# Another order of units in a fused attention, MoE and FFN kernel, with both opening AV products of a head pair at its first AV unit

## The chip, the cores and the metric

The kernel runs on one core of a Trainium2 chip. The metric is the device time of one execution in microseconds: the median of three executions of the kernel before is 460.26 us (459.25, 460.26 and 460.54). The profile is of one further execution.

The engines are TensorE (PE; its weight loads are listed apart as PEld), VectorE (DVE), ScalarE (ACT), GpSimd (POOL) and SyncE (SP), which here only issues DMA transfers. Each works through its own list of instructions in order; between lists, semaphores order the work. A DMA that SP issues has the engine name SPq in the trace, one that ScalarE issues ACTq.

## The reference

Three layers follow each other. Attention: 2 batches of 8 heads, 768 tokens of 64 dimensions; a key takes part in a query's softmax only where both have the same six-bit hash, and the bits are signs of projections.

```
q_bits = (einsum('bhsd,dk->bhsk', q, proj) > 0);  k_bits likewise
mask   = q_bucket[:, :, :, None] == k_bucket[:, :, None, :]
scores = where(mask, scale * q @ k.T, -1e9)
attn   = exp(scores - max) / (sum + 1e-09);   out = attn @ v
```

Then a soft mixture of experts on the 1536 x 512 result (8 experts with 4 slots each, `w1` 512 x 1024 and `w2` 1024 x 512 per expert, softmax of `x @ phi` over the tokens and over the slots), and a feed-forward layer `h = x @ w_in; g = h - tanh(h); g @ w_out` with 2048 hidden columns.

## The kernel before

Attention goes over the heads in eight pairs, `i` = 0 to 7. Each pair is cut into small units of work, and each unit is one Python function that issues its instructions on all the engines it needs. What is written first is first on every engine: the program's order is five lists of unit names. START runs once ahead of the pair loop, FIRST in the pass of pair 0, STEP in passes 1 to 5, STEP2 in pass 6, LAST in pass 7; the lists MOE, RUN and LOOP that follow are not touched. A pass of the loop finishes one pair and begins the next two, by a fixed offset for each unit name.

The units that matter here, with their lines:

- `const.0` (L169) loads the table `ct`, which also holds the identity matrix; `const.1` (L172) loads `proj` on ScalarE's DMA queue and two small things; `h0` to `h3` (L381) copy the queries and keys of a pair, where `xq` and `xk` have been loaded, into QA and KA.
- `b0` computes the hash bits of a pair: TensorE products L355, VectorE L361. `wk..` and `wq..` put them into QA and KA (ScalarE L369, VectorE L371). `l0` to `l3` make the low parts KB and QB (for pairs behind the first on VectorE, L419).
- `m` is one chunk of the pass that finds each query's largest masked score: TensorE `pm` (L447), then a VectorE maximum (L449). There are 18 per pair. `fa`, `fb` (or `f2` for both at once) close it: VectorE L454, a TensorE transpose `pc` (L457), VectorE L460 and L461, and a DMA that puts the row into QA. The scores of the pair need that row.
- `s0` and `s1` are chunks of scores for one head of the pair: TensorE `pst` (L508, two matmuls per block, QA with KA and QB with KB), ScalarE's exponential `e` (L511), and on GpSimd (for one head of the last pair VectorE) the running sum `es` (L521, L523).
- `a` is one AV unit: products of `e` and the values (L538) into the two tiles `pav`, of 512 and of 256 columns. Nine units belong to a pair. The first product into a tile is a constant product of `zrw` and `vzw` that sets the whole tile (L532); the tile of 512 columns gets it in the first unit, the one of 256 columns in the third.
- `xr`, `x2` and `x3` (L552, L574, L603) bring the result of a pair into its place; `lg` makes the MoE's logits of a pair (TensorE L617, VectorE L620, GpSimd L626 and L627).
- `wl` loads a piece of `w_in`, `wc` converts one: ScalarE L184, and VectorE L188, L197, L202. `lp` loads one piece of the MoE's weights (L249, `w` in the trace) into a ring of slots; slots are added as the tiles of attention are given back. The loop opens the last of them when all scores have been issued, the logits of pair 6 have been made, and pair 7's AV has begun.
- `keep.n` issues n small TensorE products (L720, `warm`) that nobody reads; each shows as two records.

All tiles in PSUM for scores, maxima and small products come from one pool of six buffers.

Of the kernel before, what the change touches and what calls it, by code (L numbers as in the profile page):

```python
# [10 lines left out]
F32 = mybir.dt.float32  # L11
# [8 lines left out]
B, H, S, D = 2, 8, 768, 64  # L20
# [4 lines left out]
P = 128  # L25
# [34 lines left out]
PARTS = ((0, 512), (512, S))  # L60
# [5 lines left out]

START = ("oi.0 qk.0 h1.0 const.1 const.0 warm.4 const.2 keep.1 hp3.0 keep.3 h0.0 wl.0 b0.0 wk0a.0 hp2.0 kc.0 wq0v.0 wl.0 "
        "m.0 keep.1 m.0 m.0 qk.1 l1.0 m.0 wk1a.0 m.0 m.0 m.0 m.0 keep.1 m.0 v.0 wq1a.0 m.0 keep.3 m.0 m.0 keep.3 m.0 "  # L70
        "v1.0 d.0 h2.1 h3.1 l0.0 m.0 fa.0 m.0 m.0 m.0 h1.1 v.1 oi.1 keep.1 b0.1 m.0 l3.0 fb.0 h0.1 wc.0 wq0a.1 wl.0 "
        "kc.1 s0.0 keep.1 l2.0 oi.2 wl.0 qk.2 fz.0 wk1a.1 s0.0 wk0v.1 s0.0 wc.0 a.0 wq1a.1 s0.0 v2.0 wc.0 s0.0 s0.0").split()
FIRST = ("wc wc lp lp a a a a a a a g0 g1 h1 fy wl m vy g2 l0 a a l1 l2 s0 h0 s0 s1 m m s1 s1 v m wl m h3 qk m m d m m "
        "xe s1 h2 b m m s0 m e wl lg m s1 m s1 m s0 lp e s0 wl xr v1 lp m x3 x2 m s1 s0 s1 e m s1 lp lp s0 s0 f2 s0 s0 "
        "wc s1 e").split()
STEP = ("a a a a a a a a wc a d g0 l0 fy h1 g1 wc l1 g2 h0 h3 lp l2 vy m m wl s0 m lp s0 s1 v xe m m qk m s0 m e xr b m "
        "h2 x2 m m v1 wl s0 lp m s1 lp s0 m m lg x3 s1 m m s1 m s0 m wc e s0 s0 s1 s1 s1 m wl s0 s1 s0 lp lp e s1 f2 e "
        "s1 wl").split()
STEP2 = ("m m a a a a a a vy s0 a a a a fy g1 l1 m s0 s0 m a m s1 h1 m s0 s1 m m m s1 g0 wl m xe d l0 xr m m v s0 v1 a a "
        "e s1 g2 m l2 a a m lp m e e lp lp s0 wl s1 wl lp b x2 qk wc s1 m m s0 v2 e lp m s1 wc h2 a a a f2 wc h3 lp h0 "  # L80
        "fz lp s0 wl s0 s1 x3 s1 lg lp").split()
LAST = ("a a s0 a lp xe a a a s0 lp lp a a lp s0 s0 lp s0 s1 s1 s0 s1 xr s0 s1 s1 lp s1 s1 lp a a lp a s0 x2 s1 s0 lg "
        "x3 s1 a").split()


MOE = ("k.1 k.1 k.1 F.0 F.1 R.1 T.0 R.0 W.0 F.2 X.0 W.1 T.2 k.1 T.1 k.1 wm.2 R.2 H.0 F.3 wm.3 X.1 k.1 T.3 W.2 H.1 X.2 "
# [55 lines left out]
def body(ctx: ExitStack, tc: tile.TileContext, q, k, v, proj, phi, w1, w2, w_in, w_out, cst, out, dbg=None):  # L142
    nc = tc.nc
    const = ctx.enter_context(tc.tile_pool(name="const", bufs=1))
# [6 lines left out]
    lg = const.tile([P, B * KT, NS], F32, name="lg")  # L151
# [101 lines left out]
    def attention():  # L253
# [23 lines left out]
        pav_p = actx.enter_context(tc.tile_pool(name="pav_p", bufs=1, space=PSUM, reuse_waits="tile"))  # L277
# [34 lines left out]
        mx, zr, vz, es, pav, xtu, rsT, rinv, uses = {}, {}, {}, {}, {}, {}, {}, {}, {}  # L312
# [213 lines left out]
        def av_unit(i, n, e2):  # L526
            cs = SEQ[n]
            k, (c0, c1) = len(cs) - 1, PARTS[len(cs) - 1]
            if cs[0] == 0:
                if k == 0:  # L530
                    pav[i] = [pav_p.tile([P, w], F32, tag=f"pav{w}", name="pav") for w in (512, S - 512)]
                nc.tensor.matmul(pav[i][k], vz[i], zr[i].rearrange("r c j -> r (c j)")[:, c0:c1], start=True, stop=False,  # L532
                                 skip_group_check=True)
                if k == 1:
                    del zr[i], vz[i]
            for j, c in enumerate(cs):
                for h in ((k + j) % 2, (k + j + 1) % 2):
                    nc.tensor.matmul(pav[i][k][64 * h:64 * h + 64, :], tv[i][:, h, c, :], e2[h][:, j * 256:j * 256 + c1 - c0],  # L538
                                     start=False, stop=c == KT - 1, tile_position=(0, 64 * h), skip_group_check=True)
# [160 lines left out]
        def unit(w, i):  # L700
# [15 lines left out]
            elif w in ("warm", "keep"):  # L716

                w_ = 256 if w == "warm" else P
                for _ in range(i):
                    nc.tensor.matmul(wt[0][:32, :w_], wz[:, :32] if w == "warm" else ident[:, :32], wz if w == "warm" else ident, start=True, stop=True)  # L720
            elif w == "b0":
                bits0(i)
            elif w[:2] in ("wq", "wk"):
                rows0(i, "qk".index(w[1]), int(w[2]), w[3:])
            elif w == "lp":
                if i > 4:
                    load_pieces(1)
            elif w == "const":
                (lambda: consts(projb), lambda: consts2(phiB, projb, blk), lambda: consts3(phiB))[i]()
            elif w in ("s0", "s1"):  # L730
                s_next(i, int(w[1]))
            elif w == "a":
                if queue and queue[0][2][1] is not None:
                    av_unit(*queue.popleft())
            elif w == "ap":
                while queue and queue[0][0] < i:
                    av_unit(*queue.popleft())
            elif w == "e":
                if len(d0.get("n", ())) < 4 and {("x3", 3), ("lg", 3)} <= done:
                    d0.setdefault("n", []).append(i)  # L740
                    disp0(len(d0["n"]) - 1)
            else:
                units[w](i)
# [3 lines left out]
        nc.vector.memset(wz, 0.0)  # L747
        for w in START:
            u, n = w.split(".")
            unit(u, int(n))  # L750
        del wt[:]
        for i in range(NPR):
            for u in FIRST if i == 0 else STEP if i <= WIDE else STEP2 if i < last else LAST:
                n = i + role.get(u, role.get(u[0], 0))
# [30 lines left out]
        while queue:  # L785
            av_unit(*queue.popleft())
# [547 lines left out]
    with tc.manual_schedule():  # L1334
# [20 lines left out]
        r = nc.values_load(flag, min_val=0, max_val=1)  # L1355
# [58 lines left out]
```

## Time and profile before

| | |
|---|---|
| median of 3 executions | 460.26 us |
| profiled execution: device time, span | 460.77 us, 459.0 us |
| TensorE busy | 437.5 us, 95% of the span |
| VectorE, ScalarE, GpSimd busy | 325.5, 272.9, 286.5 us |
| mean granted TensorE clock | 0.976 |

The span is what the trace covers; 1.77 us of the device time lie outside it. The program's stretches are: up to 10.6 us loads and the hash bits of pair 0; to 28.3 us its maxima; to 53.2 us its scores along with the maxima of pair 1; to 244.8 us the rest of the pair loop; then the MoE to some 306 us, while its weights stream in; then the feed-forward layer to the end. A window row gives, for a stretch, the busy time of each engine with its number of instructions, the granted TensorE clock as a share of full speed, the share of the DMA engines' time and the GB/s moved.

### The profile page before, as it was taken

How to read it: one execution, taken by the hardware profiler on the slowest of the kernel's cores; microseconds unless marked ns; L12 is line 12 of the kernel's file. 1: busy time of each engine (PE TensorE's matmuls, PEld its weight loads, DVE VectorE, ACT ScalarE, POOL GpSimd, SP SyncE). 2: the span in 40 equal slices, each digit the busy share in tenths (PEclk: the TensorE clock that was granted, in tenths of full speed). 3: DMA queues.
4: the chain of work that ended last, by engine and by line, in shares of the span. 5: the costliest groups of instructions: out<-in, count | busy, mean ns of one | idle time of the engine just before them, and what ended most of it. 6: DMA issues, size and time to landing. Idle time of an engine off the chain costs nothing. (4 is left out here: it accounts for less than half of the span.)

```text
span 459.0 us, 7553 instructions
## 1 busy us (share of the span) xinstructions
PE 437.5 (95%) x2621; PEld 300.1 (65%) x2621; DVE 325.5 (71%) x585; ACT 272.9 (59%) x525; POOL 286.5 (62%) x287
## 2 busy tenths in 40 slices
PE   6877999999999999999999999999999999999994
PEld 2544568575866768466766444657777778888883
DVE  3789999999999888276354358489998976444541
ACT  4568747667695756355631111288988878665751
POOL 5399849889797968949870100046878774535350
PEclk9678999999999999999999999999999999999999
DMA  6736372636455270846649999990000003000004
GB/s 180 189 116 199 84 211 88 180 95 158 143 145 174 59 196 21 311 156 272 231 191 423 416 421 420 417 413 17 2 0 3 0 0 139 0 2 0 1 2 144
DMA packets 18166, 71.33 MB, mean 155 GB/s; under 512 B 3492, under 2 KB 4616, under 8 KB 13000
## 3 DMA queue, kind: packets, MB, share of 16 engines
q1 hardware_dynamic: 17976, 70.75, 44.3%
q8 instruction: 23, 0.38, 0.4%
q14 instruction: 23, 0.19, 0.1%
q10 hardware_dynamic: 144, 0.02, 0.0%
HBM read 60.09 MB, written 3.15 MB: 138 GB/s over the span
## 5 line engine op out<-in xcount | busy, mean ns | idle before, releaser
L511 ACT ACTIVATE e<-pst 128x512 f32<-128x512 f32 x144 | 78.5, 604 | 39.0 <-PE pst L508 36.1
L521 POOL TENSOR_TENSOR es<-es,e 128x512 f32<-128x512 f32 x73 | 93.6, 1293 | 3.3 <-ACT e L511 2.5
L449 DVE TENSOR_REDUCE mx<-pm 128x1 f32<-128x512 f32 x144 | 89.7, 679 | 7.0 <-PE pm L447 6.8
L508 PE MATMUL pst<-QA,KA 128*128 128x256 f32 (+1 forms) x192 | 66.3, 359 | 3.9 <-ACT QA L369 1.3
L538 PE MATMUL pav<-e,tv 128*64 128x512 f32 (+1 forms) x384 | 66.6, 491 | 0.0
L508 PE MATMUL pst<-QB,KB 128*128 128x256 f32 (+1 forms) x192 | 63.1, 343 | 0.0
L447 PE MATMUL pm<-KA,QA 96*128 96x512 f32 x192 | 55.2, 381 | 3.8 <-DVE QA L371 3.0
L1229 DVE SCALAR_TENSOR_TENSOR ph<-win,ph 128x512 f32<-128x512 f32 (+1 forms) x64 | 35.7, 558 | 32.3 <-ACT win L1224 30.9
L1260 POOL TENSOR_TENSOR split<-win,split 128x512 fp32r<-128x512 f32 x31 | 44.6, 1439 | 14.5 <-ACT split L1255 14.5
L521 POOL TENSOR_TENSOR es<-e 128x512 f32<-128x512 f32 x30 | 39.4, 1313 | 19.6 <-PE pr L552 19.5
L1281 PE MATMUL po<-w,split 128*128 128x512 f32 x128 | 51.0, 398 | 0.0
L1279 PE MATMUL po<-w,split 128*128 128x512 f32 x128 | 50.6, 396 | 0.0
L1280 PE MATMUL po<-w,split 128*128 128x512 f32 x128 | 50.4, 394 | 0.0
L1260 POOL TENSOR_TENSOR ghl<-win,ghl 128x256 fp32r<-128x256 f32 x32 | 24.3, 758 | 37.0 <-ACT ghl L1255 37.0
L447 PEld LDWEIGHTS pm<-KA,QA 96*128 96x128 f32 x192 | 35.2, 207 | 18.5 <-issue 9.3
L538 PEld LDWEIGHTS pav<-e,tv 128*64 128x64 f32 x384 | 25.7, 136 | 31.4 <-issue 24.8
L508 PEld LDWEIGHTS pst<-QA,KA 128*128 128x128 f32 x192 | 36.9, 192 | 13.5 <-ACT e L511 5.0
L1224 ACT ACTIVATE win<-ph 128x512 f32<-128x512 f32 (+1 forms) x64 | 30.8, 481 | 22.7 <-PE ph L1217 22.1
L1230 DVE SCALAR_TENSOR_TENSOR win<-win,ph 128x512 f32<-128x512 f32 (+1 forms) x64 | 35.5, 555 | 9.1 <-ACT win L184 0.5
L1225 ACT ACTIVATE win<-win,ct 128x512 f32<-128x512 f32 (+1 forms) x64 | 39.6, 619 | 2.1
L508 PEld LDWEIGHTS pst<-QB,KB 128*128 128x128 f32 x192 | 37.1, 193 | 3.1
L1281 PEld LDWEIGHTS po<-w,split 128*128 128x128 f32 x128 | 24.0, 188 | 7.8 <-POOL split L1260 2.8
(230 smaller groups left out, 814.0 us busy)
## 6 DMA issues: line engine op xcount, KB each, us to landing
w<-in_moe_w_dram SPq DMA_DIRECT2D x32, 1024.0 KB
raw<-in_moe_w_in_dram SPq DMA_DIRECT2D x16, 512.0 KB
w<-in_moe_w_out_dram SPq DMA_DIRECT2D x8, 1024.0 KB
xq<-in_q_dram SPq DMA_DIRECT2D x8, 384.0 KB
xk<-in_k_dram SPq DMA_DIRECT2D x8, 384.0 KB
tv<-in_v_dram SPq DMA_DIRECT2D x8, 384.0 KB
out_dram<-win SPq DMA_DIRECT2D x12, 256.0 KB
QB<-QA SPq DMA_DIRECT2D x10, 192.0 KB
```

The lines of the kernel that those rows point to most:

```text
L447: nc.tensor.matmul(pm[:, j * 256:j * 256 + c1 - c0], QA[s][h][:96, c * P:(c + 1) * P], KA[s][h][:96, c0:c1], start=True, stop=True)
L449: nc.vector.reduce_max(m, pm.rearrange("p (c k) -> p c k", c=len(cs)), axis=AX.X)
L508: nc.tensor.matmul(pst[:, j * 256:j * 256 + c1 - c0], K[h][:, c * P:(c + 1) * P], Q[h][:, c0:c1], start=x == 0, stop=x == 1)
L511: nc.scalar.activation(e, pst, AF.Exp, scale=0.125)
L521: eng.tensor_tensor(q[0], y, e, ALU.add)
L538: nc.tensor.matmul(pav[i][k][64 * h:64 * h + 64, :], tv[i][:, h, c, :], e2[h][:, j * 256:j * 256 + c1 - c0], start=False, stop=c == KT - 1 ...
L1225: nc.scalar.activation(w, z, AF.Square, bias=ct[:, C_QA:C_QA + 1])
L1229: nc.vector.scalar_tensor_tensor(self.ph[p], z, Q_C, self.ph[p], ALU.mult, ALU.mult)
L1260: (eng or nc.gpsimd).tensor_tensor(gl[p], g, gh[p].bitcast(F32), ALU.subtract)
L1279: nc.tensor.matmul(po, gh[p][:, us], wo.half(f, 0), start=f == 0, stop=False)
L1280: nc.tensor.matmul(po, gh[p][:, us], wo.half(f, 1), start=False, stop=False)
L1281: nc.tensor.matmul(po, gl[p][:, us], wo.half(f, 0), start=False, stop=f == NF - 1)
```

## The change

All five lists are written in another order. Each holds the same units as before. In the AV unit, both constant products now stand in the first unit of a pair, one behind the other, instead of in the first and the third. Lines behind L530 move up by two (the AV products are L536, the logits L615, `keep` L718). Two lines of a list show the kind of edit; the other lists change alike.

```diff
-START = ("oi.0 qk.0 h1.0 const.1 const.0 warm.4 const.2 keep.1 hp3.0 keep.3 h0.0 wl.0 b0.0 wk0a.0 hp2.0 kc.0 wq0v.0 wl.0 "
...
+START = ("const.0 oi.0 qk.0 hp3.0 warm.4 const.1 const.2 b0.0 wl.0 h1.0 h0.0 hp2.0 wk0a.0 wq0v.0 keep.1 wl.0 m.0 wk1a.0 "
...
-LAST = ("a a s0 a lp xe a a a s0 lp lp a a lp s0 s0 lp s0 s1 s1 s0 s1 xr s0 s1 s1 lp s1 s1 lp a a lp a s0 x2 s1 s0 lg "
-        "x3 s1 a").split()
+LAST = ("a a a a lp xe a s0 s0 lp a a a s0 lp s0 s1 s1 s1 s0 lp xr s0 a a lp x2 x3 s1 s1 lp s1 s0 s0 s0 lp s1 s1 s1 lg "
+        "lp a a").split()
...
-            if cs[0] == 0:
-                if k == 0:
-                    pav[i] = [pav_p.tile([P, w], F32, tag=f"pav{w}", name="pav") for w in (512, S - 512)]
-                nc.tensor.matmul(pav[i][k], vz[i], zr[i].rearrange("r c j -> r (c j)")[:, c0:c1], start=True, stop=False,
-                                 skip_group_check=True)
-                if k == 1:
-                    del zr[i], vz[i]
+            if n == 0:
+                pav[i] = [pav_p.tile([P, w], F32, tag=f"pav{w}", name="pav") for w in (512, S - 512)]
+                for p, (r0, r1) in zip(pav[i], PARTS):
+                    nc.tensor.matmul(p, vz[i], zr[i].rearrange("r c j -> r (c j)")[:, r0:r1], start=True, stop=False, skip_group_check=True)
+                del zr[i], vz[i]
```

The lists of instructions that come of it differ on every engine. TensorE, the maxima of pair 0: the products of the hash bits (`pb`), the maxima (`pm`), the products that nobody reads (`warm`) and the first transpose (`pc`), before:

```order
L355 MATMUL pb<-xk,projb 32x384 x2
L447 MATMUL pm<-KA_135,QA_131 128x512
L720 MATMUL warm<-ct 32x128
L447 MATMUL pm<-KA_135,QA_131 128x512
L447 MATMUL pm<-KA_135,QA_131 128x256 x2
L447 MATMUL pm<-KA_135,QA_131 128x512 x2
L447 MATMUL pm<-KA_135,QA_131 128x256 x2
L447 MATMUL pm<-KA_135,QA_131 128x512 x2
L720 MATMUL warm<-ct 32x128
L447 MATMUL pm<-KA_135,QA_131 128x256 x2
L447 MATMUL pm<-KA_135,QA_131 128x512
L720 MATMUL warm<-ct 32x128 x3
```

And now, the same stretch:

```order
L355 MATMUL pb<-xk,projb 32x384 x2
L718 MATMUL warm<-ct 32x128
L447 MATMUL pm<-KA_135,QA_131 128x512 x2
L447 MATMUL pm<-KA_135,QA_131 128x256 x2
L447 MATMUL pm<-KA_135,QA_131 128x512 x2
L718 MATMUL warm<-ct 32x128 x6
L447 MATMUL pm<-KA_135,QA_131 128x256 x2
L718 MATMUL warm<-ct 32x128
L447 MATMUL pm<-KA_135,QA_131 128x512 x2
L718 MATMUL warm<-ct 32x128
L447 MATMUL pm<-KA_135,QA_131 128x256 x2
L718 MATMUL warm<-ct 32x128 x3
```

Up to the close of pair 0's maxima, nine of these small products stood behind `pb` before, and 13 do now, six of them in one row.

VectorE, the stretch behind the close of pair 0's maxima, as a difference; `cl` and `win` are a conversion of `w_in`, KA_136 the bit rows of pair 1:

```order
 L197 SCALAR_TENSOR_TENSOR cl<-cg,cl 128x512
 L202 SCALAR_TENSOR_TENSOR win<-raw,cl 128x512
+L493 TENSOR_TENSOR vt<-pv,blk 4x128
 L371 TENSOR_SCALAR KA_136<-pb,ct 24x384 x2
-L188 TENSOR_SCALAR cl<-raw 128x512
-L197 SCALAR_TENSOR_TENSOR cl<-cg,cl 128x512
-L202 SCALAR_TENSOR_TENSOR win<-raw,cl 128x512
-L493 TENSOR_TENSOR vt<-pv,blk 4x128
 L188 TENSOR_SCALAR cl<-raw 128x512
 L197 SCALAR_TENSOR_TENSOR cl<-cg,cl 128x512
```

Three conversions stood ahead of the close of pair 1's maxima, two stand there now; the third is made with the rest of them in pass 5.

TensorE where a pair's AV begins (here pair 0), before:

```order
L457 MATMUL pc_602<-ct_61,mh_600 12x128
L532 MATMUL pav_616<-zrw_129,vzw_130 128x512
L538 MATMUL pav_616<-e_328,tv_228 64x512
L538 MATMUL pav_616<-e_443,tv_228 64x512
L538 MATMUL pav_616<-e_348,tv_228 64x512
L538 MATMUL pav_616<-e_455,tv_228 64x512
L532 MATMUL pav_617<-zrw_129,vzw_130 128x256
L538 MATMUL pav_617<-e_464,tv_228 64x256
```

And now:

```order
L457 MATMUL pc_594<-ct_61,mh_592 12x128
L532 MATMUL pav_610<-zrw_129,vzw_130 128x512
L532 MATMUL pav_611<-zrw_129,vzw_130 128x256
L536 MATMUL pav_610<-e_328,tv_198 64x512
L536 MATMUL pav_610<-e_437,tv_198 64x512
L536 MATMUL pav_610<-e_340,tv_198 64x512
L536 MATMUL pav_610<-e_452,tv_198 64x512
L536 MATMUL pav_611<-e_490,tv_198 64x256
```

The constant product of 256 columns has moved from between two AV units to behind the other constant product. In passes further on, where scores and AV units alternate, the lists also gather AV units into longer rows.

## Rows read from the trace of the kernel before

**Rows 1.** Stretches, core 0; engine busy us (instructions), granted clock, DMA share, GB/s.

```profile
28.30:53.20 24.90, 19.91 (x84) 13.05 (x83) 23.56 (x41) 19.65 (x35) 22.93 (x19) 0.88 0.56 163
53.20:244.80 191.60, 190.83 (x1251) 126.51 (x1251) 148.53 (x272) 115.90 (x220) 155.19 (x157) 1.00 0.52 167
79.43:105.56 26.13, 26.13 (x168) 17.86 (x167) 24.46 (x45) 18.26 (x35) 22.84 (x24) 1.00 0.51 144
239.50:306.00 66.50, 63.98 (x607) 34.22 (x602) 36.53 (x68) 15.27 (x35) 7.02 (x18) 1.00 1.01 417
```

**Rows 2.** VectorE's groups, 28.3 to 53.2 us; count, busy us, mean ns, idle before.

```profile
L197 DVE SCALAR_TENSOR_TENSOR cl<-cg,cl 128x512 uint32<-128x512 uint32 x3 | 2.1, 696 | 0.5 <-ACT cg L184 0.3
L202 DVE SCALAR_TENSOR_TENSOR win<-raw,cl 128x512 uint32<-128x512 uint32 x3 | 2.1, 686 | 0.1
L188 DVE TENSOR_SCALAR cl<-raw 128x512 uint32<-128x512 uint32 x3 | 2.0, 681 | 0.0
```

**Rows 3.** One stretch of pass 5, columns as in the first group.

```profile
180.00:186.00 6.00, 6.00 (x37) 5.20 (x36) 3.60 (x8) 5.39 (x11) 5.56 (x6) 1.00 0.49 173
```

**Rows 4.** ScalarE's timeline, start: start us, duration us, instruction, idle before.

```profile
3.72 0.84 ACT L381 ACTIVATE QA<-xq 64x768 fp32r<-64x768 f32 x1 [1.71 <-DMA xq<-in_q_dram]
3.72 0.37 ACTq L172 DMA_DIRECT2D projb<-in_proj_dram  x1
4.70 0.85 ACT L381 ACTIVATE KA<-xk 64x768 fp32r<-64x768 f32 x1
```

**Rows 5.** TensorE's timeline, start of the program.

```profile
6.39 0.71 PE L355 MATMUL pb<-xq,projb 128*32 128x384 f32 x1
```

**Rows 6.** TensorE's timeline and one stretch, in the maxima of pair 0.

```profile
19.43 1.34 PE L720 MATMUL warm<-ct 128*32 128x128 f32 x6
10.24:20.48 10.24, 9.89 (x31) 6.33 (x32) 8.33 (x14) 6.36 (x9) 1.56 (x3) 0.50 0.91 241
```

**Rows 7.** TensorE's timeline, pair 1 ahead of and in its first AV units.

```profile
100.19 0.41 PE L447 MATMUL pm<-KA,QA 96*128 96x512 f32 x1
100.44 0.29 PE L508 MATMUL pst<-QA,KA 128*128 128x256 f32 x1
100.57 0.28 PE L508 MATMUL pst<-QB,KB 128*128 128x256 f32 x1
...
105.56 0.47 PE L532 MATMUL pav<-zrw,vzw 128*128 128x512 f32 x1
105.96 1.94 PE L538 MATMUL pav<-e,tv 128*64 128x512 f32 x8
107.83 0.39 PE L532 MATMUL pav<-zrw,vzw 128*128 128x256 f32 x1
108.15 1.08 PE L538 MATMUL pav<-e,tv 128*64 128x256 f32 x8
```

**Rows 8.** TensorE's weight loads in the same AV units.

```profile
106.45 0.14 PEld L538 LDWEIGHTS pav<-e,tv 128*64 128x64 f32 x2 [0.29 <-issue]
106.88 0.14 PEld L538 LDWEIGHTS pav<-e,tv 128*64 128x64 f32 x2 [0.29 <-issue]
```

**Rows 9.** TensorE's timeline, a maximum ahead of the small products of `x2`.

```profile
119.69 0.50 PE L447 MATMUL pm<-KA,QA 96*128 96x512 f32 x1
120.03 0.49 PE L574 MATMUL prt<-ct,rsT 128*128 128x128 f32 x3
```

**Rows 10.** GpSimd, SP's queue and TensorE around the weight stream's restart and end.

```profile
233.83 1.72 POOL L521 TENSOR_TENSOR es<-es,e 128x512 f32<-128x512 f32 x1
236.73 0.60 POOL L626 TENSOR_TENSOR lgt<-lgt 128x192 f32<-128x192 f32 x1 [1.18 <-DVE lgt L620]
...
238.03 2.48 SPq L249 DMA_DIRECT2D w<-in_moe_w_dram  x5
...
294.72 1.07 PE L1000 MATMUL po<-w,hold 128*32 128x256 f32 x16 [0.36 <-DMA w<-in_moe_w_dram]
```

**Rows 11.** TensorE's longest wait, 53.2 to 244.8 us: releaser, us, times, longest.

```profile
PE pc L457 <- DVE mh L454: 0.9, 1, 0.9
```

More of the change, by code (lines that the diff above doesn't have):

```diff
@@ L65 @@
 RING, HOLD = (4, 1, 3, 4, 3, 2, 3, 1), 4
-START = ("oi.0 qk.0 h1.0 const.1 const.0 warm.4 const.2 keep.1 hp3.0 keep.3 h0.0 wl.0 b0.0 wk0a.0 hp2.0 kc.0 wq0v.0 wl.0 "
-        "m.0 keep.1 m.0 m.0 qk.1 l1.0 m.0 wk1a.0 m.0 m.0 m.0 m.0 keep.1 m.0 v.0 wq1a.0 m.0 keep.3 m.0 m.0 keep.3 m.0 "
-        "v1.0 d.0 h2.1 h3.1 l0.0 m.0 fa.0 m.0 m.0 m.0 h1.1 v.1 oi.1 keep.1 b0.1 m.0 l3.0 fb.0 h0.1 wc.0 wq0a.1 wl.0 "
-        "kc.1 s0.0 keep.1 l2.0 oi.2 wl.0 qk.2 fz.0 wk1a.1 s0.0 wk0v.1 s0.0 wc.0 a.0 wq1a.1 s0.0 v2.0 wc.0 s0.0 s0.0").split()
@@ L73 @@
[L73 to L78, printed above, removed]
@@ L79 @@
-STEP2 = ("m m a a a a a a vy s0 a a a a fy g1 l1 m s0 s0 m a m s1 h1 m s0 s1 m m m s1 g0 wl m xe d l0 xr m m v s0 v1 a a "
-        "e s1 g2 m l2 a a m lp m e e lp lp s0 wl s1 wl lp b x2 qk wc s1 m m s0 v2 e lp m s1 wc h2 a a a f2 wc h3 lp h0 "
-        "fz lp s0 wl s0 s1 x3 s1 lg lp").split()
-LAST = ("a a s0 a lp xe a a a s0 lp lp a a lp s0 s0 lp s0 s1 s1 s0 s1 xr s0 s1 s1 lp s1 s1 lp a a lp a s0 x2 s1 s0 lg "
-        "x3 s1 a").split()
+START = ("const.0 oi.0 qk.0 hp3.0 warm.4 const.1 const.2 b0.0 wl.0 h1.0 h0.0 hp2.0 wk0a.0 wq0v.0 keep.1 wl.0 m.0 wk1a.0 "
+        "kc.0 m.0 m.0 v.0 m.0 m.0 keep.3 l0.0 keep.3 m.0 keep.1 m.0 wq1a.0 m.0 qk.1 keep.1 h2.1 oi.1 h3.1 m.0 keep.3 "
+        "m.0 wl.0 l1.0 m.0 d.0 m.0 v1.0 keep.1 fa.0 m.0 m.0 m.0 v.1 b0.1 l3.0 m.0 m.0 h0.1 m.0 fb.0 h1.1 wl.0 wc.0 "
+        "wk1a.1 wq1a.1 s0.0 l2.0 fz.0 wq0a.1 s0.0 v2.0 kc.1 qk.2 s0.0 wk0v.1 keep.1 oi.2 wc.0 s0.0 a.0 wc.0 s0.0 s0.0").split()
@@ new lines @@
+FIRST = ("a a a a a a a wc lp fy g0 g1 m l0 l1 wc lp a wl m a vy g2 s0 h1 l2 h3 h0 v qk s1 s0 m s1 m xe d h2 m s0 m m e "
+        "wl s1 m xr wl v1 m s1 m m s0 b lg m s0 m s1 s1 m m s0 e s0 s0 m s1 x2 e m e wl lp s1 lp m s1 x3 f2 lp s0 lp wc "
+        "s1 s0").split()
+STEP = ("d a wc g0 a l0 g1 wc a a l1 h1 fy h0 a a a g2 lp a a l2 h3 vy m wl m s0 s0 m lp m s1 xe m s0 m v m qk e xr b m "
+        "h2 s0 x2 v1 m m s0 m s1 m m wl lg x3 lp s1 lp m s1 m m s0 wc s0 s1 s0 m lp e s1 m s1 s0 s1 e s1 lp wl f2 wl s0 "
+        "e s1").split()
@@ L86 @@
+STEP2 = ("a a m m a g1 a fy a a a a l1 a m s0 vy s0 a m a m s0 m s1 s1 m h1 s0 m xe g0 m l0 m xr m v a a lp wl e v1 lp "
+        "g2 d lp s1 wl m e s0 l2 m a s1 e m wc s0 x2 v2 s1 wl s0 s0 h0 m m qk b wc e lp m lp s1 lp s1 wc s1 m lp a a a "
+        "h3 a f2 fz s0 s1 wl x3 lg h2 lp").split()
+LAST = ("a a a a lp xe a s0 s0 lp a a a s0 lp s0 s1 s1 s1 s0 lp xr s0 a a lp x2 x3 s1 s1 lp s1 s0 s0 s0 lp s1 s1 s1 lg "
+        "lp a a").split()
 MOE = ("k.1 k.1 k.1 F.0 F.1 R.1 T.0 R.0 W.0 F.2 X.0 W.1 T.2 k.1 T.1 k.1 wm.2 R.2 H.0 F.3 wm.3 X.1 k.1 T.3 W.2 H.1 X.2 "
```

## The prediction
> **What bounds the kernel now.** I read the windows by stage first, then the waits of TensorE in the longest stage, then single rows where the order of units changes. The windows [rows 1] show stages with different limits. From 28.3 to 53.2 us VectorE is busy 23.56 of 24.90 us, TensorE only 19.91: an instruction taken off VectorE there is time. From 53.2 to 244.8 us TensorE is busy 190.83 of 191.60 us at full clock, and the longest wait in it is one of 0.9 us, for VectorE at the close of a pair [rows 11]: there only the cost of TensorE's own instructions counts, that is, who stands beside whom. From 239.5 to 306 us the DMA engines are busy throughout, at 417 GB/s, with the MoE's weights, while TensorE still has 63.98 of 66.50 us of work; near the end it waits 0.36 us for a weight [rows 10]. So the MoE sits on the edge of both, and what counts is when the stream restarts, 238.03 us, in relation to the end of attention. What comes behind is not touched.
>
> The sum is made against the profiled execution, 460.77 us (span 459.0 us, 1.77 outside it), which is 0.51 us above the median of 460.26; I take the differences over to the median.
>
> **A. One conversion leaves the VectorE-bound stage: -2.1 us.** VectorE had three conversions ahead of the close of pair 1's maxima and now has two. One costs 0.681 + 0.696 + 0.686 = 2.06 us [rows 2]. VectorE is 95% busy there, so nearly all of it comes out of the path; the least would be 0.7 (if the 1.34 us that VectorE is idle now come on top), the most 2.1. I take 2.1, because the idle pieces of VectorE lie at waits that the new order keeps. What is late next is TensorE, 19.91 of 24.90, far behind. The conversion goes to pass 5, where VectorE is busy 3.60 of 6 us [rows 3], so beside TensorE's work: 0. If that cover were gone it would cost the same 2.1 again.
>
> **B. The start: +0.5 us.** Two edits work against each other. `proj` is issued at 3.72 now, behind a copy for which ScalarE waited 1.71 us; it goes first, so the hash products, at 6.39 [rows 4, 5], can start when the keys have landed, which is by 4.70, when the key copy starts [rows 4]. That is at most -1.7. I take half of it, -0.8, since the rows don't show when the keys land, nor what the earlier products wait for in their turn. Against it, four more of the products that nobody reads (eight records) stand within the maxima of pair 0, six of them (twelve records) in one row. Six records take 1.34 us at the granted clock of 0.50 there [rows 6], so eight cost 1.34 x 8 / 6 = 1.8, and TensorE is busy 9.89 of 10.24 us in that stretch, so hardly any lies in a gap. Walked through unit by unit the row that the scores need comes some half microsecond later than now; I take +0.5. The ends: +1.8 if the earlier `proj` brings nothing, and -1.7 - 1.9 = -3.6 if it brings all and the 1.91 us in which VectorE idles in the window of [rows 6] go too, which needs the full clock earlier.
>
> That window is where a rule of the Trainium skill speaks against the small products. TensorE was busy 97% of it and yet was granted half the clock throughout [rows 6]. The Trainium skill, "TensorE: Matmul & The Clock Gate", section "What's actually happening", says that "the default state is throttled, and activity releases the throttle"; by that, more small products would bring the full clock sooner, and B would come near its lower end. The trace does not bear that out here, since a stretch of nearly unbroken activity stayed throttled.
>
> **C. Both constant products at the first AV unit: -1.9 us.** A plain 512-column product next to another starts 0.25 us before the next (100.19 to 100.44), one of 256 columns 0.13 (100.44 to 100.57) [rows 7]. The constant products, each between other kinds, take 0.40 (105.56 to 105.96) and 0.32 (107.83 to 108.15). The AV products between them have a cadence of 0.43 for two records (106.45 to 106.88) [rows 8], so the last four should take 0.86, and take 0.95 up to the second constant product (106.88 to 107.83): 0.09 for that change. So now 0.40 + 0.09 + 0.32 = 0.81. Afterwards the first has its like behind it, 0.25, the second an AV product, 0.32, and there is no change out of AV: 0.57. That is 0.24 a pair, 1.9 for eight. Ends: 0, if the price hangs on the tile and not on the neighbour, and (0.81 - 0.25 - 0.13) x 8 = 3.4 if the second costs as little as a plain product. It all lies in the stage that TensorE bounds. The tile of 256 columns is now needed one AV unit earlier; it came free with the pair before, so I add nothing.
>
> **D. Other neighbours on TensorE: -0.5 us.** Where the small products of `x2` follow a maximum, the step takes 0.34 us (119.69 to 120.03) [rows 9], against 0.25 above; the new lists avoid that at five places, 5 x 0.09 = 0.5. AV units also stand in longer rows. Ends: 0 and -1.5.
>
> **E. The weight stream restarts later against attention: +1.0 us.** SP issues the first load at 238.03, when GpSimd has made the logits of pair 6; ahead of it GpSimd idled 1.18 us, behind the last `es` addition of 1.72 us [rows 10]. In the new LAST, the scores of pair 7 all stand ahead of the logits: four score products of 256 columns that stood behind now come first, 4 x 0.13 = 0.5 [rows 7], and one more `es` addition is queued in front, 1.72 - 1.18 = 0.5 beyond the gap. Ends: 0, and 0.5 + 2 x 1.72 - 1.18 = 2.8 with two additions in front. As the stream is at the DMA engines' limit until the last MoE weight, this comes through to the end.
>
> At nothing I cost the other moves on ScalarE, GpSimd, SP and its loads: in a pair ScalarE is busy 18.26 and GpSimd 22.84 of 26.13 us [rows 1], and the DMA share is 0.51. Uncovered, each late `es` addition would stop scores for up to 1.72 us.
>
> Sum: -2.1 + 0.5 - 1.9 - 0.5 + 1.0 = -3.0. The profiled execution would take 457.8, the median 457.3 us. All ends at once would give -2.1 - 3.6 - 3.4 - 1.5 + 0 = -10.6 and -0.7 + 1.8 + 0 + 0 + 2.8 = +3.9; taken as independent of each other (the root of the squares of their distances) they reach 4.6 below the forecast and 3.2 above it.
>
> **Rivals.** (1) *The clock recovers sooner.* If TensorE gets its full clock before 20 us, B is -0.8 - 1.9 = -2.7 in place of +0.5: 457.3 - 3.2 = 454.1. For it: the products begin sooner and are more. Against it: a busy share of 97% did not do it before. This is the one to which the rule above leads.
>
> (2) *The MoE takes the gain back.* If the additions in front of the logits are two (E at 2.8), the restart of the stream moves hardly at all, and attention's gain turns into a wait for weights: 457.3 + 1.8 = 459.1; with A at its small end, 460.5. For it: all nine score units stand in a row there, and GpSimd's additions are slower than TensorE's scores. Against it: GpSimd idled before this logits addition. The result is no change.
>
> (3) *VectorE runs short in the pair loop: slower.* A pair takes 26.13 us, of which VectorE works 24.46 [rows 1]; with C and D the period shrinks to about 25.8 and leaves VectorE 1.3 us idle. If the new STEP bunches maxima, so that VectorE waits 3.0 us in each (as by the 0.9 us at the close of a pair [rows 11], three times over), the period is 24.46 + 3.0 = 27.5, 1.7 above 25.8, in four passes +6.6: 457.3 + 6.6 = 463.9. It decides from an idle of about 2.1 us a pair, where 4 x 0.8 eats the 3.0. For it: 94% busy, in a list that is new throughout. Against it: the units alternate as finely as before, and PSUM's six buffers carry a few units of slack.
>
> **How the numbers follow.** The forecast, 457.3 us, has a chance of 0.52, with its own range 455.3 to 458.8; rival (1) 0.14, (2) 0.15, (3) 0.19. A measurement here tells about 0.3% (1.4 us) from no change: faster is under 458.9, slower above 461.6. Faster: 0.52 less a little for its upper edge, plus 0.14, plus a little of (2): 0.66. Same: 0.15. Slower: 0.19. The range leaves out about half of (1) below 453.8 and most of (3) above 462.2.
>
> **What would show it.** A: three conversions' instructions fewer between the pairs' closes, and the first AV product near 53.4 - 2.1 + 0.5 = 51.8 us. B: `pb` near 5 to 5.6 us, and when the granted clock reaches 1.00. C: the first two L532 in a row, the second 0.12 to 0.32 long, and pairs of about 25.8 us between first AV products. E: the first stream load 5.8 us before attention's end, in place of 6.8 now (238.03 to 244.8), and longer waits for `w` at L1000. Wrong would be new waits of TensorE on VectorE or ScalarE in the pair loop, or a MoE that ends at the same time as before.

## The result, and the profile after

The changed kernel takes 454.51 us (median of four, 454.35 to 455.70) against 460.03 us of the kernel before (459.25 to 460.54); the ratio is 0.9892, with a 95% interval of 0.9870 to 0.9914. That is 5.5 us less, where 3.0 were forecast. The time lies within the whole range of the prediction, 453.8 to 462.2, but below the forecast's own 455.3 to 458.8: it is at the place of rival (1), 454.1.

The marks of the stages, read from the timelines of the profiled executions. *First maximum* is the start of the first L447, *close* the start of the second L461 (the row that pair 0's scores need), *first AV* the first constant product L532, *attention's end* the first small product of the last `x2`, *restart* the first load of the weight stream behind its pause, *feed-forward* the first `ph`.

| kernel | first maximum | close | first AV | attention's end | restart | feed-forward | span |
|---|---|---|---|---|---|---|---|
| before | 10.59 | 28.06 | 53.41 | 244.84 | 238.03 | 299.33 | 459.0 |
| after | 9.37 | 25.44 | 48.95 | 237.95 | 232.09 | 293.27 | 452.6 |
| after, a second profile (e5) | 9.98 | 26.34 | 50.59 | 239.51 | 233.64 | 294.86 | 454.5 |
| e1, START alone | 10.09 | 26.48 | 50.80 | 242.41 | 235.60 | 296.78 | 456.2 |
| e2, all but START | 9.79 | 25.99 | 51.85 | 240.35 | 234.50 | 295.73 | 454.9 |
| e3, AV unit alone | 9.85 | 27.17 | 52.30 | 242.32 | 235.51 | 296.79 | 456.3 |
| e4, two conversions | 10.34 | 27.68 | 51.86 | 243.17 | 236.35 | 297.59 | 457.1 |
| e6, head of START alone | 9.63 | 25.86 | 51.24 | 242.64 | 235.83 | 297.03 | 456.8 |
| e7, START from the first maximum on alone | 10.51 | 27.79 | 50.63 | 242.19 | 235.37 | 296.48 | 455.8 |
| e8, after, no small products in the maxima | 9.96 | 25.06 | 48.58 | 237.54 | 231.68 | 292.81 | 451.9 |
| e9, before, no small products in the maxima | 10.08 | 25.01 | 51.78 | 242.49 | 235.68 | 296.78 | 456.4 |
| e10, logits early | 9.61 | 24.83 | 48.10 | 238.95 | 226.71 | 292.89 | 452.6 |
| e12, logits between | 10.10 | 25.12 | 48.62 | 237.62 | 230.49 | 291.69 | 450.9 |

From the first two lines: 4.46 us come from the start (2.62 up to the close, 1.84 from there to the first AV), 2.43 from there to attention's end (191.43 to 189.00), and 0.83 are given back in the MoE (54.49 to 55.32). The second profile of the same kernel has 2.82 in the start: executions differ by a microsecond or two there. The START of before shows it too: in the four profiles that have it up to the close (before, e2, e3, e4) the close stands at 25.99 to 28.06. The profile of before is the latest of them, so differences to it in the start are on the large side.

Windows of the kernel after, columns as in [rows 1]; the first three are the thirds of the stretch of [rows 6], then VectorE's stretch, the pair loop, and the MoE from restart to feed-forward:

```profile
10.24:13.65 3.41, 3.41 (x17) 2.33 (x15) 2.80 (x5) 2.38 (x4) 3.35 (x5) 0.59 1.02 282
13.65:17.07 3.42, 3.42 (x18) 1.97 (x18) 2.58 (x4) 0.00 (x0) 3.21 (x4) 0.91 1.10 285
17.07:20.48 3.41, 1.94 (x15) 1.30 (x17) 2.77 (x7) 1.63 (x3) 0.64 (x2) 1.00 0.51 117
25.70:48.95 23.25, 19.25 (x85) 13.34 (x84) 21.96 (x38) 18.20 (x33) 19.42 (x19) 0.88 0.50 152
48.95:237.95 189.00, 188.78 (x1251) 126.65 (x1251) 148.00 (x275) 115.66 (x220) 154.23 (x155) 1.00 0.53 170
232.09:293.27 61.18, 58.48 (x553) 31.05 (x545) 30.43 (x53) 9.29 (x22) 4.45 (x16) 1.00 1.00 409
```

The granted clock is the first thing to see: where [rows 6] had 0.50 throughout, it is 0.59, 0.91 and 1.00. VectorE's stretch is 23.25 us with 21.96 busy, in place of 24.90 with 23.56 [rows 1]: shorter by about what VectorE no longer does. TensorE is as busy in the pair loop as before, and the loop is shorter.

TensorE's timeline of the kernel after, start of the program (answering [rows 4 and 5]) and the maxima:

```profile
4.25 0.89 PE L355 MATMUL pb<-xq,projb 128*32 128x384 f32 x4
5.64 0.52 PE L355 MATMUL pb<-xk,projb 128*32 128x384 f32 x2 [0.50 <-DMA xk<-in_k_dram]
9.37 1.40 PE L447 MATMUL pm<-KA,QA 96*128 96x512 f32 x6 [2.89 <-POOL zrw L303]
10.70 2.63 PE L718 MATMUL warm<-ct 128*32 128x128 f32 x12
...
15.88 0.84 PE L718 MATMUL warm<-ct 128*32 128x128 f32 x6
```

The queries' bits start at 4.25, the keys' at 5.64, when the keys land; no wait for `proj` shows. Six records of the small products take 0.84 us at 15.88, against 1.34 in [rows 6].

TensorE's timeline and weight loads where a pair's AV begins, answering [rows 7 and 8]:

```profile
100.51 0.59 PE L532 MATMUL pav<-zrw,vzw 128*128 128x512 f32 x2
101.02 3.23 PE L536 MATMUL pav<-e,tv 128*64 128x512 f32 x18
```

```profile
101.50 0.14 PEld L536 LDWEIGHTS pav<-e,tv 128*64 128x64 f32 x2 [0.28 <-issue]
101.93 0.14 PEld L536 LDWEIGHTS pav<-e,tv 128*64 128x64 f32 x2 [0.28 <-issue]
102.36 0.14 PEld L536 LDWEIGHTS pav<-e,tv 128*64 128x64 f32 x2 [0.29 <-issue]
102.79 1.01 PEld L536 LDWEIGHTS pav<-e,tv 128*64 128x64 f32 x10 [0.29 <-issue]
```

Both constant products together take 101.02 - 100.51 = 0.51 us, and the AV products behind them keep the cadence of 0.43 over the place where the second one stood. GpSimd and SP's queue at the restart, answering [rows 10]:

```profile
228.35 1.26 POOL L521 TENSOR_TENSOR es<-e 128x512 f32<-128x512 f32 x1
229.57 1.26 POOL L521 TENSOR_TENSOR es<-es,e 128x512 f32<-128x512 f32 x1
230.80 0.59 POOL L624 TENSOR_TENSOR lgt<-lgt 128x192 f32<-128x192 f32 x1
231.47 0.59 POOL L625 TENSOR_TENSOR lg<-lg,lgt 128x192 f32<-128x192 f32 x1
...
232.09 10.49 SPq L249 DMA_DIRECT2D w<-in_moe_w_dram  x8
```

The logits addition has no idle time ahead of it any more: it stands behind an `es` addition, and the loads leave when it is done.

### The profile page after: what moved, and what is told of

Read it like the earlier page. It is cut to its first block, busy times and chain, and to the rows that moved or that the text cites. A ratio compares the mean times of both kernels' runs of the same rounds, so it can differ in the third digit from the quotient of the medians.

```text
span 452.6 us, 7545 instructions
## 1 busy us (share of the span) xinstructions
PE 430.2 (95%) x2621; PEld 298.6 (66%) x2621; DVE 323.4 (71%) x585; ACT 272.5 (60%) x525; POOL 285.5 (63%) x287
## 5 line engine op out<-in xcount | busy, mean ns | idle before, releaser
L536 PE MATMUL pav<-e,tv 128*64 128x512 f32 (+1 forms) x384 | 65.0, 489 | 0.0
L447 PE MATMUL pm<-KA,QA 96*128 96x512 f32 x192 | 52.7, 361 | 3.6 <-POOL zrw L303 2.9
L536 PEld LDWEIGHTS pav<-e,tv 128*64 128x64 f32 x384 | 26.3, 137 | 33.6 <-issue 27.3
L447 PEld LDWEIGHTS pm<-KA,QA 96*128 96x128 f32 x192 | 32.3, 195 | 15.9 <-DVE mx L449 3.9
```

Source lines behind the costliest of these rows:

```text
L447: nc.tensor.matmul(pm[:, j * 256:j * 256 + c1 - c0], QA[s][h][:96, c * P:(c + 1) * P], KA[s][h][:96, c0:c1], start=True, stop=True)
```

## The experiments

Each was timed beside the kernel before on one chip; times are medians, ratios carry their 95% interval. The ratio is not the quotient of the two medians and differs from it by up to 0.0018 (0.8 us). The expectations give times counted from some 460 us, while the kernel before took 459.88 to 461.26 us beside the experiments, so the gain is the safer thing to compare. The first question is where the gain is; the second, why the start gained where a loss was forecast; the third, what the weight stream costs.

**e1, START alone.** The list START of the kernel after, all else before.

```diff
-START = ("oi.0 qk.0 h1.0 const.1 const.0 warm.4 const.2 keep.1 hp3.0 keep.3 h0.0 wl.0 b0.0 ...
+START = ("const.0 oi.0 qk.0 hp3.0 warm.4 const.1 const.2 b0.0 wl.0 h1.0 h0.0 hp2.0 wk0a.0 ...
```

> The kernel before with the new START alone; the other lists and the AV unit as before. Theory (the start earns more than the passes: hash products earlier, full clock earlier, one conversion fewer): the first AV product stands near 49.0 us in place of 53.4, the passes take the 191.4 us that they took, and the time is 460.0 - 4.5 = 455.5. Rival (the start's gain hangs on the new FIRST behind it, or is handed back at the weight stream): the first AV product above 50.5, the time above 457.5.

457.38 against 460.58 us, ratio 0.9922 (0.9894 to 0.9950): 3.2 us. The time is just under the rival's bound of 457.5 and far from the theory's 455.5, and the first AV product came at 50.80, on the rival's side, not at 49.0: the one profile from which the theory took its number was a favourable one. The rival's reason is not seen, though: the passes take 191.60 us (191.43 before), and the restart stands as before against attention's end.

**e2, all but START.** The kernel after with the START of before.

```diff
-START = ("const.0 oi.0 qk.0 hp3.0 ...
+START = ("oi.0 qk.0 h1.0 const.1 ...
```

> The kernel after with the old START. Theory: the first AV product stays near 53.4, first AV product to the end of attention takes 189.0 in place of 191.4, the weight stream restarts 0.95 us later against the end of attention, so the time is 460.0 - 2.4 + 0.95 = 458.6, between 458.0 and 459.2. Rival (the orders of the passes carry most of the gain): below 457.

458.04 us against 460.58, ratio 0.9932 (0.9905 to 0.9959): at the lower edge of the theory's band, not the rival's, though 2.5 us under the kernel before beside it. The passes take 188.50, the restart is 5.85 us ahead of attention's end (6.81 before). e1 and e2 together give 3.2 + 2.5 = 5.7, against 5.5 for the whole change: the two parts add up, within intervals of over a microsecond on each.

**e3, the AV unit alone.** All lists old.

```diff
-            if cs[0] == 0:
...
+            if n == 0:
+                pav[i] = [...]
+                for p, (r0, r1) in zip(pav[i], PARTS):
+                    nc.tensor.matmul(p, vz[i], ...[:, r0:r1], start=True, stop=False, ...)
```

> The kernel before with the changed AV unit alone, all lists old. Theory (price by neighbours, 0.24 us a pair): 460.0 - 1.9 = 458.1. Rival (the constant product costs the same wherever it stands, and the 2.4 us of the passes come from the lists): 459.7 to 460.3.

458.06 us against 460.58, ratio 0.9953 (0.9922 to 0.9985), as the theory has it. In the marks only 1.41 of it lie in the passes (190.02 us, 191.43 before); another 1.11 lie ahead of the first AV product, where nothing was changed, so the agreement of the time is in part luck. The times between first AV products show the saving by pair: 25.68, 25.82, 25.79, 26.53 and 27.41 us, against 26.02, 26.13, 26.10, 26.84 and 27.76, so 0.31 to 0.35 less each. In the sixth it turns: 17.87 against 17.32. Its timeline names a wait that the kernel before does not have:

```profile
191.31 0.47 PE L508 MATMUL pst<-QA,KA 128*128 128x512 f32 x1 [1.54 <-DMA QA<-row]
```

The row of the next pair, which goes through a DMA, was late for the faster TensorE. In the kernel after, with its other order of units, that wait does not occur.

**e4, two conversions.** Before, with the last two loads of `w_in` in START left out, so that its third `wc` finds nothing to convert; what is missing is loaded and converted in pass 5.

```diff
-... fb.0 h0.1 wc.0 wq0a.1 wl.0 kc.1 s0.0 keep.1 l2.0 oi.2 wl.0 qk.2 ...
+... fb.0 h0.1 wc.0 wq0a.1 kc.1 s0.0 keep.1 l2.0 oi.2 qk.2 ...
```

> The kernel before, with two loads of w_in fewer in START, so that its third conversion finds nothing and two conversions in place of three stand ahead of the close of pair 1's maxima. Theory (VectorE bounds that stretch): the close moves 1.8 to 2.1 us earlier, the time is 458.0 to 458.4. Rival (the conversion fills idle time of VectorE, or the clock falls in another place): 459.3 or more.

459.13 us, ratio 0.9963 (0.9939 to 0.9988): 1.5 us, between the two. From close to first AV it is 24.18 in place of 25.35. One conversion of 2.06 us is worth 1.2 to 1.5 here, not all of it.

**e5 to e8, what the start gained by.** The whole change again; then the head of START new with the old maxima (e6), the old head with the new maxima (e7), and the kernel after without the small products between the first maximum and the close (e8).

```diff
 e6: START = after's units up to the first "m.0" + "kc.0" + before's from the first "m.0" on
 e7: START = before's units up to the first "m.0" + after's from there on
 e8, in after's START:
-... m.0 m.0 keep.3 l0.0 keep.3 m.0 keep.1 m.0 wq1a.0 m.0 qk.1 keep.1 ... keep.3 m.0 ... keep.1 fa.0 ...
+... m.0 m.0 l0.0 m.0 m.0 wq1a.0 m.0 qk.1 ... m.0 ... fa.0 ...
```

> The kernel after once more, beside the others of this call. Theory: its mean granted clock is 0.983 to 0.987 where the kernel before has 0.972, about 11 us less of half clock, and its time is 5.0 to 6.0 below that of before. Rival (the clock of its first profile was chance): a clock of 0.972 to 0.976 and less than 4.5 below.

> The kernel before with only the head of START new (order of loads and first copies, hash products ahead of the small products), the maxima of pair 0 in the old order with five small products fewer than the kernel after has. Theory (the long row of small products in the maxima brings the full clock): the clock stays at 0.971 to 0.976, the hash products come 1.2 us earlier, the time is 459.2 to 459.8. Rival (the head decides, as it lets the unbroken work begin sooner): a clock of 0.980 or more and a time of 458.3 or less.

> The kernel before with the old head of START and all that follows in START new (the long row of small products, and two conversions in place of three). Theory: a clock of 0.980 or more, and 460.6 - 1.5 for the conversion - 1.4 for the clock = 457.7. Rival (the head decides): a clock of 0.971 to 0.976 and 459.0 or more.

> The kernel after without the small products that nobody reads between the first maximum and the close of pair 0's maxima. Theory: the clock falls back to 0.971 to 0.976 and the time is 1 to 2 us above that of the kernel after. Rival (the small products cost time and bring nothing): the clock stays at 0.983 or more and the time is 0.5 to 1.7 below that of the kernel after.

| | us | ratio (interval) | median granted clock |
|---|---|---|---|
| before, beside these | 461.26 | | 0.972 |
| e5, after again | 455.96 | 0.9878 (0.9840 to 0.9916) | 0.979 |
| e6, new head | 458.98 | 0.9960 (0.9933 to 0.9987) | 0.976 |
| e7, new maxima | 457.36 | 0.9917 (0.9892 to 0.9942) | 0.986 |
| e8, no small products | 453.77 | 0.9840 (0.9804 to 0.9875) | 0.976 |

e5 repeats the gain (5.3 us); its clock, 0.979, is above that of before, a little under the band expected. e6 and e7 decide between head and maxima for the clock: it rises with the new maxima (0.986), not with the head (0.976). By time the head brings 2.3 us and the new maxima, with the conversion, 3.9; for e6 both expectations were off, the clock going with the theory, while the time of 458.98 lies between the two bands. The two do not add up: together they are e1's START, which brought 3.2, not 6.2. What makes them overlap is not traced. e8 then takes the theory's point away. Without the small products the clock falls back to 0.976, as the theory said, and yet the kernel is 2.2 us faster than after, as the rival said. The two profiles have nearly the same first maximum (9.98 and 9.96). VectorE's timeline with the small products (e5):

```profile
10.57 3.08 DVE L449 TENSOR_REDUCE mx<-pm 128x1 f32<-128x512 f32 x5
14.84 2.65 DVE L449 TENSOR_REDUCE mx<-pm 128x2 f32<-128x512 f32 x4 [1.19 <-PE pm L447]
17.81 1.89 DVE L449 TENSOR_REDUCE mx<-pm 128x1 f32<-128x512 f32 x3 [0.32 <-PE pm L447]
19.73 0.17 DVE L454 TENSOR_REDUCE mh<-mx 128x6 f32<-128x12 f32 x1
```

and without them (e8), with its window:

```profile
10.64 7.27 DVE L449 TENSOR_REDUCE mx<-pm 128x1 f32<-128x512 f32 x12
17.93 0.17 DVE L454 TENSOR_REDUCE mh<-mx 128x6 f32<-128x12 f32 x1
```

```profile
10.24:20.48 10.24, 7.37 (x27) 5.18 (x28) 9.50 (x19) 4.47 (x7) 7.52 (x11) 0.50 0.89 238
```

Twelve maxima follow each other without a gap at a granted clock of 0.50. The half clock alone does not hold VectorE up; the small products between the score products do.

**e9, the same on the kernel before.**

```diff
-... m.0 keep.1 m.0 m.0 qk.1 ... keep.1 m.0 v.0 wq1a.0 m.0 keep.3 m.0 m.0 keep.3 m.0 ... keep.1 b0.1 ...
+... m.0 m.0 m.0 qk.1 ... m.0 v.0 wq1a.0 m.0 m.0 m.0 m.0 ... b0.1 ...
```

> The kernel before without the small products that nobody reads between the first maximum and the close of pair 0's maxima; all else as before. Theory (at half clock they hold up the maxima, and so VectorE, which idled 0.60 + 0.95 + 0.84 us behind them): the close comes 1.5 to 2.4 us earlier at a clock that is no higher, the time is 1.5 to 2.4 below that of before. Rival (they keep the half-clock time short, and without them the whole start runs at half clock): the same time as before or longer.

457.59 against 460.34 us, ratio 0.9937 (0.9915 to 0.9958): 2.75 us less at a clock of 0.971, which was 0.972 before. From first maximum to close it takes 14.93 us, with the small products 17.47. VectorE's maxima with them (before):

```profile
12.68 5.47 DVE L449 TENSOR_REDUCE mx<-pm 128x1 f32<-128x512 f32 x9 [0.60 <-PE pm L447]
19.11 1.29 DVE L449 TENSOR_REDUCE mx<-pm 128x1 f32<-128x512 f32 x2 [0.95 <-PE pm L447]
21.23 1.29 DVE L449 TENSOR_REDUCE mx<-pm 128x1 f32<-128x512 f32 x2 [0.84 <-PE pm L447]
```

and without (e9):

```profile
10.67 8.46 DVE L449 TENSOR_REDUCE mx<-pm 128x1 f32<-128x512 f32 x14
```

The theory holds, though not all of the gain lasts: from the close to the first AV product it takes 26.77 us, 1.42 more than before.

**e10, logits early.** e8, with pair 6's logits behind its `x3` and the last scores of head 0 in front of those of head 1.

```diff
-LAST = ("... lp x2 x3 s1 s1 lp s1 s0 s0 s0 lp s1 s1 s1 lg lp a a").split()
+LAST = ("... lp x2 x3 lg s0 s0 s0 lp s1 s1 lp s1 s1 s1 s1 lp a a").split()
```

> The kernel after without the small products in the maxima, and with pair 6's logits moved up in LAST, ahead of the last seven score units (and the three of head 0 ahead of the four of head 1). Theory (the end of the MoE follows the restart of the weight stream by 61.2 us, whatever attention does): the restart comes 2 to 4 us earlier against attention, the time falls by 1.0 to 2.5 against the same kernel with the old place (453.8), until TensorE is the limit of the MoE. Rival (attention's end sets the MoE, the stream is early enough): within 0.5 of 453.8.

454.37 against 460.34 us, ratio 0.9882 (0.9858 to 0.9906): no gain on e8 (0.9840), a miss for the theory as far as time goes. The restart came 12.24 us ahead of attention's end, 6.4 earlier than in e8 where 2 to 4 were expected, and the MoE took 53.94 us from there, 1.3 less than in e8 (55.27); but attention lost 1.9 (190.85 from first AV in place of 188.96). Its timeline shows 1.0 of that:

```profile
232.18 0.51 PE L550 MATMUL pr<-es,ones 128*32 128x384 f32 x1 [1.01 <-POOL es L521]
```

The logits now stood ahead of `es` additions on GpSimd, and TensorE's sums waited for these. The other 0.9 is not traced.

**e11, no small products at all.** e8 without the two remaining ones of START.

> The kernel after without any of the small products on the table, also the one ahead of the maxima and the one among pair 0's scores. Theory (they only cost): 0.2 to 0.6 below the kernel without those in the maxima (453.8). Rival (some are wanted for the clock of the next stretch): 0.5 or more above it.

453.88 us, ratio 0.9878 (0.9854 to 0.9903): within 0.2 us of e8's median, so neither; these two cost nothing that shows. (Against the kernel before beside each, e11 gains 6.5 us and e8 7.5; the intervals overlap.)

**e12, logits between.** e8, with the logits behind the scores of head 0 and ahead of the last three of head 1, and four AV units ahead of the sums.

```diff
-LAST = ("... s1 s0 s0 s0 lp s1 s1 s1 lg lp a a").split()
+LAST = ("... s1 s0 s0 s0 lg lp s1 s1 s1 lp a a a a").split()
```

> The kernel after without the small products in the maxima, with pair 6's logits behind the scores of head 0 and ahead of the last three score units of head 1, and two more AV units ahead of the last sums so that they cover GpSimd's additions. Theory (the stream's restart bounds the MoE, and the wait of the sums for GpSimd took back what the earlier logits brought): the restart comes 0.8 to 1.5 us earlier against attention, TensorE waits under 0.3 us for the sums, and the time is 0.4 to 1.2 below 453.8. Rival (the MoE takes no less, or the wait comes back): within 0.4 of 453.8 or above.

452.54 against 459.88 us, ratio 0.9838 (0.9807 to 0.9869), 1.2 us under e8's median. GpSimd's logits stand ahead of the last `es` addition, and the AV units cover that:

```profile
229.20 0.60 POOL L624 TENSOR_TENSOR lgt<-lgt 128x192 f32<-128x192 f32 x1
229.88 0.59 POOL L625 TENSOR_TENSOR lg<-lg,lgt 128x192 f32<-128x192 f32 x1
230.43 1.27 POOL L521 TENSOR_TENSOR es<-es,e 128x512 f32<-128x512 f32 x1
```

The restart is at 230.49, 7.13 us ahead of attention's end, which is at 237.62 as in e8. Its median is the lowest of all. Against the kernel before beside it, it gains no more than e8 (ratio 0.9838 against 0.9840), so that it beats e8 is not shown by the times; what shows the step is the marks, in one profile each: from attention's end to the feed-forward layer 54.07 us in place of 55.27, after the same first AV.

## Why the prediction was right or wrong

**A, the conversion: right in kind, somewhat large.** Forecast -2.1; e4 gives -1.5 in time and -1.2 in the marks, the kernel after -1.84 from close to first AV. Over the profiles that stretch takes 25.12 to 25.86 with three conversions (before, e2, e3, e6; e9 is apart) and 22.84 to 24.32 with two (after, e1, e4, e5, e7), 1.6 less on the mean. VectorE bounds that stretch, as said: both its busy time and the stretch fell by about 1.6. In pass 5 the conversion lies beside TensorE's work, as said: from pair 4's first AV to pair 5's it takes 27.07 us, where it took 27.76; with the conversion moved and nothing else (e4) it takes 27.88, so 0.1 of it shows.

**B, the start: wrong, in sign.** Forecast +0.5; measured -2.6 and -1.7 at the close in two profiles. Those are differences to the latest of four closes of the old START: from mean to mean (before, e2, e3, e4 against after, e1, e5) it is -1.1. By time START alone gained 3.2 (e1), of which e4 gives 1.5 to the conversion, so -1.7 is left for B.

The first half of the step, hash products earlier, held in direction: the first maximum stands at 9.37 to 10.10 in the eight profiles with the new head and at 9.79 to 10.59 in the six with the old one, 0.4 earlier on the mean, against 0.8 taken. Its reason is not borne out. In the kernel before the hash products start at 6.39 directly behind small products that had waited for `ct`:

```profile
5.11 1.46 PEld L720 LDWEIGHTS warm<-ct 128*32 128x32 f32 x8 [1.19 <-DMA ct<-in_const_dram]
6.39 0.13 PEld L355 LDWEIGHTS pb<-xq,projb 128*32 128x32 f32 x1
```

In e2, with the same START, `proj` was issued no earlier (3.76) and the hash products started at 5.81. So `proj` was not what held them until 6.39.

The step that failed is "so eight cost 1.8, and TensorE is busy 9.89 of 10.24 us in that stretch, so hardly any lies in a gap". It took the price of a small product from rows at half clock and held the clock fixed. In the kernel after the granted clock reached 1.00 within the maxima, six records cost 0.84 instead of 1.34, and from first maximum to close it took 16.07 and 16.36 us, not 17.47 + 1.3. (The 1.3 is what B's +0.5 leaves when its -0.8 is taken off; by its own terms, -0.8 + 1.8, it would have been +1.0. The upper reach of the range is 3.3, not 3.2; nothing hangs on either.) The profiles that bear on it, with the granted clock from 10.24 to 20.48:

| small products | profile | granted clock | first maximum to close |
|---|---|---|---|
| old order | before, e4, e3 | 0.50, 0.53, 0.54 | 17.47, 17.34, 17.32 |
| old order | e2, e6 | 0.67, 0.67 | 16.20, 16.23 |
| new order | e7 | 0.69 | 17.28 |
| new order | after, e5, e1 | 0.83, 0.83, 0.83 | 16.07, 16.36, 16.39 |
| none | e8, e9 | 0.50, 0.59 | 15.10, 14.93 |

With small products the stretch follows the clock: the same old order takes 1.1 to 1.3 less at 0.67 than at 0.50 to 0.54. At a like clock (0.67 to 0.69) the new order takes about 1.05 more than the old, near the 1.3 that the prediction charged for it, though from one profile. So the price was about right, as far as one profile tells, and the fixed clock was wrong. The single executions point the same way: straight lines through those of the kernel before with a mean clock up to 0.984 fall by 1.7 to 2.3 us for each 0.010, so the 0.983 of e1 in place of 0.972 would be worth some 2 us, an estimate. It is not the whole rule, since six executions of the kernel before with a mean clock of 0.991 to 0.995 took 461.32 to 463.70 us.

That is rival (1), with -2.7 for B and 454.1 us in all; 454.51 was measured. That it is so close is in part luck: by e1 and e4 B is -1.7, not -2.7. Its rule, in the Trainium skill, "TensorE: Matmul & The Clock Gate", section "What's actually happening", was set aside because one stretch of before, 97% busy, had stayed at half clock. The traces agree with it in part: the new order raised the clock (0.69 to 0.83, e7 and the kernel after), taking the small products out lowered it again (0.50 in e8). The kernel before is not explained by it: there the clock stayed at 0.50 for 10.24 us under as busy an engine, and the same START was granted 0.67 in e2 while less busy, 9.04 us of 10.24.

Rival (1) named the right event but not the whole ground for the time. e8 and e9 are faster yet with the clock at 0.971 to 0.976. What binds in the maxima is VectorE, 12 in 7.27 us, and TensorE feeds it at half clock as well; a small product among the score products delays a maximum, more so at half clock. Against the 15 us that the stretch takes without them, the old order lost 1.2 to 2.5 us by them and the new one 1.1 to 1.4, and 2.3 in e7. The prediction saw VectorE's idle time there and put it down to the clock, not to what stood between the maxima. How the start's gain divides between clock, order and head stays open: the division above is an estimate, and e6 and e7 do not add up to e1.

**C and D: the sum right, the split not.** Forecast -1.9 and -0.5, together -2.4; the stretch fell by 2.43. e3 shows C larger than forecast, 0.31 to 0.35 a pair instead of 0.24 (both constant products take 0.51 us, not 0.57, so 0.81 - 0.51 = 0.30), which would be 2.6 for eight, and then a wait of 1.54 for the row's DMA, so that 1.41 was left. D's saving does not show by itself: up to the sixth pair's first AV product the kernel after takes 131.47 us and e3, with the old lists, 131.23 (before 132.85); from there to attention's end it is 57.53 against 58.79, which e3's wait of 1.54 alone would cover. So the agreement of the sum is in part luck.

Rival (3), VectorE running short, did not come: TensorE is busy 188.78 of 189.00 us in the pair loop, and the first two pairs take the 25.7 to 25.8 that were forecast (the third 26.11, as before). The wait that the prediction read out of [rows 11], and multiplied for this rival, was never in the pair loop. It ends at 53.18, just ahead of the first AV product, and it stands in the same place in the kernel after, longer:

```profile
53.18 0.27 PE L457 MATMUL pc<-ct,mh 128*12 128x128 f32 x1 [0.88 <-DVE mh L454]
48.71 0.27 PE L457 MATMUL pc<-ct,mh 128*12 128x128 f32 x1 [1.12 <-DVE mh L454]
```

The longest wait in the loop of before was another, 0.65 us, which is gone:

```profile
193.50 0.47 PE L508 MATMUL pst<-QA,KA 128*128 128x512 f32 x1 [0.65 <-ACT vhi L494]
```

**E, the restart: right.** Forecast 1.0 later against attention's end; it went from 6.81 to 5.86 ahead of it, 0.95. The mechanism is the one named: one more `es` addition in front of the logits and no gap. And it comes through to the end: from restart to the feed-forward layer it is 61.30 us before and 61.18 after, and 61.0 to 61.3 in all profiles but e10, which had the stream so early that it no longer set the end: from attention's end to the feed-forward layer it took 53.94 us with the restart 12.24 ahead, hardly less than the 54.07 of e12 with 7.13 ahead. TensorE's wait for a weight near the end of the MoE grew as was said, from 0.36 us to 0.7. So rival (2) was the right place to look, with a smaller price than its 2.8.

The sum: A to E as forecast would be -3.0; with the measured -1.84, -2.62, -2.43 and +0.83 it is -6.1 in the profiles (span -6.4), and -5.5 in the medians. Nearly all of the difference to the forecast is B.

## What to carry to other kernels

Filler products that are to raise TensorE's clock must be priced by what they delay on the engine that binds, here VectorE: leaving them out gained 2 to 3 us in both orders, although the mean clock fell or stayed. Where a stream of loads runs at its limit behind a release, find the instruction that releases it and count from there, not from the end of the compute; moving that instruction up pays only as long as nothing else is queued behind it that the path waits for (e10 against e12, by their marks). A price read from rows at one clock level does not hold when the edit itself can change the level. And where one list was granted 0.50 of the clock in one execution and 0.67 in another, a single profile of before is no baseline for a difference of 2 us.

## What the hardware showed that was not expected

- TensorE's granted clock fell to half about where the maxima begin, in every profile, after a stretch in which TensorE mostly waited (TensorE was busy 0.80 us of the 3.41 ahead of it, before). How long it stayed there was not a matter of being busy alone: 0.50 over 10.24 us with TensorE busy 9.89 (before), against 0.59, 0.91 and 1.00 in the thirds of that stretch with it busy 8.77 (after), and 0.67 with it busy 9.04 under the START of before (e2).
- Executions of one kernel spread: the kernel before ran from 458.13 to 463.72 us beside e1, with mean granted clocks of 0.965 to 0.994, and the lowest clock was not the longest time (463.64 us at 0.991). e8's six lie within 453.16 to 454.26.
- Two constant products next to each other cost 0.51 us (101.02 - 100.51); apart, each between AV products, 0.81.
